# Attention with relative bias and a mixture of adapters: K and V of a head pair in one transfer each, re-aligned by GpSimd casts

## The chip, the cores and the metric

The kernel runs on one core of a Trainium2 chip. The metric is the device time of one execution in microseconds (us); the shown median is over three runs. The engines are TensorE (PE, with its weight loads as PEld), VectorE (DVE), ScalarE (ACT), GpSimd (POOL) and SyncE (SP), which here only issues transfers. The profile is one execution taken by the hardware profiler.

## The reference

Eight batches, eight heads, 576 positions, head dimension 64, all in float32. Each head's scores get a bias that depends on the distance of the two positions; the attention output, laid out as 4608 rows of 512, goes through a mixture of eight rank-16 adapters of which each row uses two.

```python
scores = scale * np.matmul(q, k.transpose(0, 1, 3, 2))
bucket = np.where(is_small, n, large)          # n = |i - j|, 32 buckets
scores = scores + bias_table[bucket].transpose(2, 0, 1)[None]
attn = np.exp(scores - scores.max(-1, keepdims=True))
attn = attn / (attn.sum(-1, keepdims=True) + 1e-09)
x = np.matmul(attn, v)                         # then (4608, 512)
logits = x @ w_gate                            # two best of 8, softmax over the two
out = x + sum(w[:, e] * ((x @ A[e]) @ B[e]) for the two chosen e)
```

## The kernel before, in words

The work goes over 32 head pairs (4 per batch). The 576 positions of a head are 512 in four tiles of 128 (the body) and 64 at the end (the tail). The two heads of a pair stand side by side in 128 columns, so that one transpose serves both; the tails of two heads stand in the two halves of the partitions.

For each pair i: K, Q and V of both heads are loaded as float32 (`kf`, `qf`, `vf`). GpSimd casts them to bfloat16 (`ck_` into `kb`, `cq_` into `qb`, `cv_` into the tiles `vn`, which have a column of ones for the row sums). PE transposes `kb` and `qb` into the PSUM tile `kqps` (`T_pe`), DVE copies it to `kqT` (`T_ev`). PE makes the scores in five parts `qk(i, c)`: four of body keys against body queries, the fifth with the tails of keys and queries, for which the bias (`Hk`, `MT`) is added by matmuls. ACT takes the exponential of each part (`softmax_exp`, 128 x 1024 in, `p` out): 160 such instructions in all. DVE multiplies the exponentials of the bias into a band around the diagonal with two instructions per pair, `p` times `M` (`band`: 128 x 1536 and 128 x 1024, called "bands" below). PE multiplies `p` with `vn` and the tail values `vt` (`pv`), DVE normalizes (`norm1`, `norm2`: `rc` and `x`).

The tails are loaded per batch: `tf` holds those of K and of Q, `vtf` those of V; GpSimd casts them into `tl` (`ct_`) and `vt` (`cvt_`), PE transposes `tl` (`tT_pe`) and makes the scores of tails against tails (`tt_pe`), ACT their exponential (`ptt`). After the fourth pair of a batch the mixture follows: transposes, projection `zf`, the gate chain (`df`, `mk`, `ex`, `sm`, `gate`, of which GpSimd does `df`, `sm`, the product with `ex` and `gate`), `zt` on GpSimd, output `o`. The last batch's mixture is written out separately (`final`), with its gate chain on DVE.

The bias comes from a table: `buckets_of` and `onehot` on DVE, a small matmul `g`, its exponential on ACT and its scaled copy on DVE into `gg`, a store to DRAM (`g_d`), and loads from there that shear it (`Mr`, four of them, and `Hk`), of which DVE makes `M` and `MT`.

Nothing runs in the order in which it is written. Each piece of work is added to a list with an engine, a planned cost in ns, what it depends on, and a due time, to which the table `OFF` adds an offset by key. A planner then lays all of it out engine by engine, earliest due time first among what could start, with planned costs and latencies, and the instructions are emitted in that order; each engine then works strictly in its order. The planner models that a band and a GpSimd instruction exclude each other (`o.sb`, `sb_free`), and it lets each GpSimd instruction wait for one of the two last DVE instructions planned ahead of it (`tie`). Its costs for the GpSimd casts are 560 ns for 512 elements a partition.

Rings of buffers: `kf`, `qf`, `vf` five each, `kb` and `qb` three, `vn` four, `vt` and `tl` two by batch.

Of the kernel before, what the change touches and what calls it, by code (L numbers as in the profile page):

```python
# [10 lines left out]
FP32 = mybir.dt.float32  # L11
# [16 lines left out]
def kernel(  # L28
# [66 lines left out]
    class Op:  # L95
# [5 lines left out]
    WARM2 = 14  # L101
    YIELD = 50
    LATE = 700
# [4 lines left out]
        "lv0": 3.3, "lt0": 28.6, "lvt0": -4.6, "lm0": -27.85, "lm1": -4.85, "lm2": -0.55, "lm3":  # L108
        -2.75, "lh": 1.85, "MT": -1.05, "M0": 4.6, "M1": -8.15, "M2": -2.45, "lw": 2.9, "lwb": -3.8,
        "cv": 11.2, "ct_": -2.35, "cvt0": -5.7, "cvt1": -0.3, "tT0": -2.4, "tT1": -14.4, "tt_":  # L110
        -0.4, "ttx_": -37.4, "qk4_": 0.95, "bd0": -8.7, "bd1": 1.7, "pv00": -6.85, "pv01": -831.15,
        "pv02": -813.15, "pv03": -768.1, "pv04": -778.35, "pv05": -11.85, "na0": -256.25, "nb0":
        -294.1, "pv10": -7.2, "pv11": -712.45, "pv12": -659.3, "pv13": -671.35, "pv14": -747.35,
        "pv15": -8.55, "na1": -52.05, "nb1": -20.35, "lq1": 0.5, "lv1": 1.25, "lt1": -0.5, "lvt1":
        -2.65, "ck": 2.25, "cq": 5.5, "Tk": -9.6, "Tq": -8.8, "Te": -231.7, "qk0": -2.95, "qk1":
        -2.7, "qk2": -7.95, "qk3": -3.95, "lk2": -6.2, "lq2": -15.45, "lv2": 2.2, "qk4": -4.9,
        "lk3": -0.2, "lq3": -1, "lv3": 1, "mx00": -6.7, "mx01": -2.9, "me0": -18, "mx10": -7.25,
        "me1": -29.1, "mt": -3.9, "mte0": -28.55, "mte1": -9.75, "zm0": -5.95, "zm1": -13.05,
        "zem0": -4.4, "zm2": -7.4, "zm3": -6.75, "zem2": -14.75, "gmxm": 37.4, "gdfm": 3.8, "gmkm":
        -9.5, "gexm": -0.4, "gsmm": -11.4, "gmem": 0.75, "grsm": -3.9, "ggtm": 2.6, "gzm0": -5.4,  # L120
        "zTm": -26.15, "zTem": -0.85, "o0": -10.7, "oe0": -23.05, "ost": 6.9, "o2": -3.25, "oe2":
        -0.7, "lq4": -0.5, "lv4": -6.8, "ct0": -2.05, "ct1": 2.35, "tt": -19.35, "ttx": 11.25,
        "lk5": -8.6, "lq5": 6.65, "lv5": 0.65, "lt": 0.15, "lvt": 9.7, "lk": 0.95, "lq": -0.7, "lv":
        0.65, "zt0": -5.25, "zet0": 0.55, "gdft": 0.35, "grst": -7.3, "ggtt": -3.15, "zTt": -13.1,
        "zTet": 1.35, "ot0": -8.95, "ot1": -11.55, "ote": -1.85, "mx00L": -7.55, "mx01L": -4.9,
        "me0L": 3.75, "mx10L": -2.15, "mx11L": -7.65, "me1L": -11, "mtL": -7.95, "mte0L": 4.45,
        "mte1L": -0.45, "zm0L": -15.45, "zm1L": 0.35, "zem0L": 12.15, "zm2L": -9.15, "zm3L": -8.35,
        "zem2L": -1.45, "gmxmL": -6.1, "gdfmL": 3.5, "gmkmL": -14.7, "gexmL": -4.4, "gsmmL": -0.5,
        "gmemL": 5.7, "grsmL": -0.25, "ggtmL": 4.25, "gzm0L": 0.5, "gzm2L": 6.45, "zTmL": -1.8,
        "o0L": 2, "ostL": -6.65, "o2L": 2, "bdL0": -1.9, "bdL1": -0.2, "pvL01": -1.55, "pvL02":  # L130
        -1.7, "pvL03": -0.75, "pvL05": 0.75, "naL0": 3.3, "nbL0": -0.1, "pvL10": -4.7, "pvL11":
        5.65, "pvL12": 1.6, "pvL13": -0.25, "pvL14": -12.7, "pvL15": -0.55, "naL1": -11.25, "nbL2":
        -19.15, "nbL3": -0.7, "fT00": -28.7, "fE00": 15.55, "fEt00": -1.5, "fEt01": -0.5, "fz0":
        0.2, "fw0": -1.45, "fT10": -1.65, "fE10": -13.6, "fEt10": -2.05, "fEt11": 0.45, "fz1": -12,
        "fw1": -4, "fT20": -31.55, "fE20": -2.65, "fEt20": 4.2, "fEt21": -12.8, "fz2": -12, "fT30":
        -39.65, "fE30": 2.65, "fT32": -15.3, "fE32": 0.55, "fEt30": 3.25, "fEt31": 0.25, "fz3": -12,
        "fw3": -4, "gdfL": -5.5, "gmkL": -3.7, "gexL": -3.65, "gsmL": -32.3, "grsL": -3.35, "ggtL":
        -3.1, "fze0": -3.4, "fze2": -0.65, "fze4": -9.95, "fx1": -0.75, "fx3": 0.15, "fx4": 1,
        "fw2": -4,
# [39 lines left out]
    bk = cp.tile([NB, 512], BF16, tag="bk")  # L179
    oneh = cp.tile([NB, 512], FP32, tag="oneh")  # L180
# [29 lines left out]
    def nat_dma(i, h, key, src):  # L210
        b, hp = divmod(i, HP)
        if h == 0:
            stg[(i, key)] = ldp.tile([128, 4, 2, D], FP32, name=key, tag=key)
        SY.dma_start(out=stg[(i, key)][:, :, h, :],
                     in_=src[b, 2 * hp + h, 0:S4, :].rearrange("(g p) d -> p g d", p=128))

    def k0_dma(h):
        if (0, "kf") not in stg:
            stg[(0, "kf")] = ldp.tile([128, 4, 2, D], FP32, name="kf", tag="kf")
        if h is None:  # L220
            AC.dma_start(out=stg[(0, "kf")][:, 0], in_=k[0, 0:2, 0:128, :].rearrange("h p d -> p h d"))
        else:
            SY.dma_start(out=stg[(0, "kf")][:, 1:4, h, :],
                         in_=k[0, h, 128:S4, :].rearrange("(g p) d -> p g d", p=128))
# [7 lines left out]
    def tail_dma(b, w, e, en):  # L232
        if w == 0 and e == 0:
            stg[(b, "tf")] = ldp.tile([128, 2, HP, D], FP32, name="tf", tag="tf", bufs=2)
        EN[en].dma_start(out=stg[(b, "tf")][e * 64:(e + 1) * 64, w],
                     in_=(k, q)[w][b, :, S4:, :].rearrange("(c e) p d -> e p c d", e=2)[e])

    def vtail_dma(b, e):
        if e == 0:
            stg[(b, "vtf")] = ldp.tile([128, HP, D], FP32, name="vtf", tag="vtf", bufs=2)  # L240
        SY.dma_start(out=stg[(b, "vtf")][e * 64:(e + 1) * 64],
                     in_=v[b, :, S4:, :].rearrange("(c e) p d -> e p c d", e=2)[e])

    def load(i):
        t0 = 5.0 * i
        nk = 0.0 if i < 2 else max(4500, 8000 + 980 * (t0 - 17))
        nv = 0.0 if i < 1 else max(8000, 8000 + 980 * (t0 - 12))
        dk = t0 - 14 if i > 5 else -76 + 8 * i if i > 1 else -88
        dv_ = t0 - 8 if i > 4 else -64 + 8 * i if i else -80
        pre = [g_("ck", i - 5), g_("cq", i - 5), g_("cv", i - 5)]  # L250
        ke = str(i) if i < 6 else ""
        if i:
            R["lk", i] = [add("SP", 505, lambda h=h: nat_dma(i, h, "kf", k), pre[:1], dk + .01 * h,
                              nb=nk, dma=600, key="lk" + ke) for h in range(2)]
        else:
            R["lk", 0] = [add("ACT" if h is None else "SP", 450, lambda h=h: k0_dma(h), (),
                              -69 if h is None else -90, dma=300 if h is None else 450)
                          for h in (None, 0, 1)]
        R["lq", i] = [add("SP", 510, lambda: q_dma(i, "SP"), pre[1:2], dk + .02 if i else -95, nb=nk,
                          dma=780, key="lq" + ke if i else None)]  # L260
        R["lv", i] = [add("SP", 505, lambda h=h: nat_dma(i, h, "vf", v), pre[2:], dv_ + .01 * h,
                          nb=nv, dma=600, key="lv" + ke) for h in range(2)]

    def loadt(b, due):
        n = 0.0 if b == 0 else 14000.0 if b == 1 else 8000 + 980 * due
        ke = str(b) if b < 2 else ""
        en = "SP" if b else "ACT"
        for w in range(2):
            for e in range(2):
                R["lt", b, w, e] = add(en, 610, lambda w=w, e=e: tail_dma(b, w, e, en), [g_("ct", b - 2)],  # L270
                                       (due if b > 1 else (-60, -45)[b]) + .01 * e, nb=n, dma=400, key="lt" + ke)
        for e in range(2):
            R["lvt", b, e] = add("SP", 610, lambda e=e: vtail_dma(b, e), [g_("cvt", b - 2)],
                                 (due + 3 if b > 1 else (-58, -34)[b]) + .01 * e,
                                 nb=n + 3000 if b else 9300, dma=400, key="lvt" + ke)

    def ck_(i, e):
        kq[(i, 0)] = ntp.tile([128, 4, 2, D], BF16, name="kb", tag="kb")
        bcopy(EN[e], kq[(i, 0)], stg.pop((i, "kf")))

    def ck0_(w):
        if w == 0:
            kq[(0, 0)] = ntp.tile([128, 4, 2, D], BF16, name="kb", tag="kb")
        s = slice(0, 1) if w == 0 else slice(1, 4)
        PL.tensor_copy(kq[(0, 0)][:, s], stg[(0, "kf")][:, s])

    def T0_pe(w):
# [3 lines left out]
        for j in ((0,), range(4), (1, 2, 3))[w]:  # L291
            PE.transpose(ps[:, w % 2, j * 128:(j + 1) * 128], kq[(0, w % 2)][:, j], ident)
# [15 lines left out]
    def ct_(b, e, h):  # L308
        z = slice(h * 64, (h + 1) * 64)
        bcopy(EN[e], tls[b % 2][z, :, :, z], stg[(b, "tf")][z])  # L310
        if h:
            stg.pop((b, "tf"))
# [935 lines left out]
```

## Time and profile before

| what | value |
|---|---|
| median of 3 runs | 210.38 us (210.02 to 212.13) |
| the profiled execution's own time | 210.69 us |
| its span, first to last instruction | 208.9 us |
| PE, DVE, ACT, POOL busy | 180.3, 171.8, 163.0, 102.9 us |
| granted clock of TensorE, mean | 0.975 |
| POOL instructions | 212 |
| DMA packets, moved | 99649, 39.82 MB |
| of these under 512 B | 87448 |
| K loads on SP | 62 of 128 KB, 4.1 us to landing (median) |
| V loads on SP | 64 of 128 KB, 3.8 us |
| Q loads on SP | 32 of 256 KB, 3.7 us |

How to read the profile: "busy" is the time in which an engine had an instruction in work; issuing transfers and waiting for semaphores are not counted. A line of groups gives source line, engine, operation, output and input tiles with their shapes, the count, the busy time in us, the mean of one in ns, the idle time of the engine just ahead of these instructions, and what ended most of it. All instructions of DVE and POOL carry line L65, that of a recording helper, so they are told apart by their tiles. A line in order of time begins with the start and the length in us; what stands in brackets is the idle time ahead of it and what ended it.

### The profile page before, as it was taken

What the parts mean: (1) busy time and instruction counts of PE and PEld (TensorE: products, weight loads), DVE (VectorE), ACT (ScalarE), POOL (GpSimd) and SP (SyncE); (2) the same over time, 40 slices, a digit from 0 to 9 for tenths busy, and PEclk for the clock granted to TensorE, in tenths of its full rate; (3) what the DMA queues carried; (4) which work ended last, traced back from release to release, by engine and by line L of the source; (5) the groups of instructions that cost most, each with busy time, mean ns of one, the idle gap of its engine ahead of it and who ended that gap; (6) DMA issues with size and microseconds to landing.
All of it is one profiled execution on the core that took longest, in us unless ns stands there. A gap on an engine that the chain in (4) does not pass through costs nothing.

```text
span 208.9 us, 7237 instructions
## 1 busy us (share of the span) xinstructions
PE 180.3 (86%) x2858; PEld 128.3 (61%) x2890; DVE 171.8 (82%) x428; ACT 163.0 (78%) x191; POOL 102.9 (49%) x212
## 2 busy tenths in 40 slices
PE   6838687999999996999998989999999999999660
PEld 3425555777667675666676656667776767669420
DVE  4218578688999979999899989999889999999760
ACT  2348489799999977798889977998989987994350
POOL 7552435646555866729546445654566563001200
PEclk9985999999999999999999999999999999999996
DMA  5949787879787998989768996799789922202057
GB/s 143 258 107 256 160 221 157 178 181 235 167 197 179 272 277 202 237 225 280 184 178 199 264 269 160 184 299 270 174 219 242 287 52 100 104 3 55 0 218 234
DMA packets 99649, 39.82 MB, mean 191 GB/s; under 512 B 87448, under 2 KB 96664, under 8 KB 99616
## 3 DMA queue, kind: packets, MB, share of 16 engines
q1 hardware_dynamic: 96656, 38.17, 71.4%
q10 hardware_dynamic: 2960, 1.20, 2.4%
q8 instruction: 22, 0.36, 0.7%
q14 instruction: 11, 0.09, 0.2%
HBM read 29.90 MB, written 9.45 MB: 188 GB/s over the span
## 4 chain that ended last, share of the span: by engine, by line
PE 40%; DVE 32%; DMA 11%; ACT 6%; issue 3%; POOL 2%; SPq 1%; ACTq 1%; POOLq 0%; DVEq 0%
DVE p L65 12%; PE pv L416 9%; PE sc L362 7%; ACT p L389 5%; PE kqps L349 5%; DVE x L65 4%; DMA kf<-in_k_dram 4%; DVE zf L65 3%; DVE kqT L65 3%; DMA Hk<-g_d 3%; PE pv L425 2%; DMA tf<-in_k_dram 2%; PE sc L567 2%; DVE xT L65 2%; PE sc L367 2%
## 5 line engine op out<-in xcount | busy, mean ns | idle before, releaser
L389 ACT ACTIVATE p<-sc 128x1024 bf16<-128x1024 f32 x160 | 151.2, 1039 | 22.9 <-PE sc L362 9.8
L65 DVE TENSOR_TENSOR p<-p,M 128x1536 bf16<-128x1536 bf16 x64 | 54.6, 853 | 2.7 <-ACT p L389 1.7
L416 PEld LDWEIGHTS <-p 128*128 128x128 bf16 x1024 | 37.8, 98 | 16.1 <-issue 6.7
L362 PE MATMUL sc<-kqT 64*128 64x512 bf16 x256 | 44.5, 396 | 3.7 <-ACT p L389 3.6
L416 PE MATMUL pv<-vn,p 128*128 128x65 bf16 x1024 | 42.6, 195 | 5.4 <-DVE kqT L65 1.6
L65 DVE TENSOR_TENSOR x<-pv,rc 128x320 bf16<-128x320 f32 (+1 forms) x65 | 31.2, 483 | 1.2
L65 POOL CAST kb<-kf 128x512 bf16<-128x512 f32 (+2 forms) x33 | 21.2, 643 | 19.9 <-DMA kf<-in_k_dram 5.1
L65 DVE COPY kqT<-kqps 128x1024 bf16<-128x1024 bf16 (+3 forms) x34 | 22.1, 653 | 7.2 <-PE kqps L349 4.7
L65 POOL CAST qb<-qf 128x512 bf16<-128x512 f32 x31 | 21.8, 702 | 10.4 <-PE sc L362 5.1
L65 POOL CAST vn<-vf 128x512 bf16<-128x512 f32 x32 | 19.7, 616 | 9.1 <-DVE p L65 2.7
L362 PEld LDWEIGHTS <-kqT 64*128 64x128 bf16 x256 | 11.3, 94 | 15.7 <-issue 7.1
L420 PE MATMUL pv<-vn,p 128*128 128x65 bf16 x256 | 18.3, 194 | 0.5 <-ACT p L389 0.5
L425 PE MATMUL pv<-vt,p 128*128 128x65 bf16 x256 | 18.3, 194 | 0.0
L65 DVE RECIPROCAL rc<-pv 128x5 f32<-128x5 f32 x64 | 12.0, 187 | 6.1 <-PE pv L425 5.6
L65 DVE TENSOR_TENSOR o<-sc,x 128x1024 f32<-128x1024 f32 x12 | 14.6, 1215 | 0.2
L349 PE MATMUL kqps<-ident,kb 128*128 128x128 bf16 x124 | 12.1, 220 | 2.7 <-DVE rc L65 1.2
L65 POOL CAST tl<-tf 64x512 bf16<-64x512 f32 x16 | 11.3, 707 | 5.7 <-DVE p L65 2.2
L425 PE MATMUL pv<-vt,ptt 128*128 128x65 bf16 x64 | 12.4, 194 | 1.0 <-ACT ptt L341 1.0
L367 PE MATMUL sc<-tlT,kqT 128*128 128x128 bf16 x128 | 12.7, 222 | 0.5 <-ACT p L389 0.4
L420 PEld LDWEIGHTS <-p 128*128 128x128 bf16 x256 | 12.2, 98 | 0.9 <-ACT p L389 0.9
L349 PEld LDWEIGHTS <-kb 128*128 128x128 bf16 x124 | 7.5, 97 | 8.3 <-DVE x L65 2.9
L425 PEld LDWEIGHTS <-p 128*128 128x128 bf16 x256 | 12.0, 98 | 0.0
(128 smaller groups left out, 268.8 us busy)
## 6 DMA issues: line engine op xcount, KB each, us to landing
qf<-in_q_dram SPq DMA_DIRECT2D x32, 256.0 KB, 3.7
vf<-in_v_dram SPq DMA_DIRECT2D x64, 128.0 KB, 3.8
kf<-in_k_dram SPq DMA_DIRECT2D x62, 128.0 KB, 4.1
out_dram<-o SPq DMA_DIRECT2D x14, 512.0 KB, 4.3
vtf<-in_v_dram SPq DMA_DIRECT2D x16, 64.0 KB, 3.4
tf<-in_k_dram SPq DMA_DIRECT2D x14, 64.0 KB, 3.4
tf<-in_q_dram SPq DMA_DIRECT2D x14, 64.0 KB, 2.9
out_dram<-ot SPq DMA_DIRECT2D x6, 128.0 KB, 2.8
```

The lines of the kernel that those rows point to most:

```text
L65: self.inst = f(*a, **k)
L349: PE.transpose(ps[:, w, j * 128:(j + 1) * 128], t[:, j], ident)
L362: PE.matmul(sc[:, h * 512:(h + 1) * 512], lhsT=t[s, 0, c * 128:(c + 1) * 128], rhs=t[s, 1, :], start=True, stop=True)
L367: PE.matmul(sc[:, g * 128:(g + 1) * 128], lhsT=t[:, 0, g * 128:(g + 1) * 128], rhs=tt[:, 1, hp, :], start=(g == 0), stop=True, skip_group_ ...
L389: AC.activation(probs[(i, c)], st.pop((i, c, "sc")), ACT.Exp, scale=scale)
L416: PE.matmul(acc[:, s, :], lhsT=p[:, o:o + 128], rhs=vn[:, part, h, :], start=(part == 1 and s == 0), stop=False, skip_group_check=True)
L420: PE.matmul(acc[:, 4, :], lhsT=p[:, g * 128:(g + 1) * 128], rhs=vn[:, g, h, :], start=False, stop=False, skip_group_check=True)
L425: PE.matmul(acc[:, s, :], lhsT=l, rhs=vt[:, hp, h * D1:(h + 1) * D1], start=False, stop=True, skip_group_check=True)
L567: PE.matmul(ps[:, k_], lhsT=st[(b, "m", "zT")][:, t + k_, :], rhs=Bb, start=True, stop=not last)
```

## The change

K of a pair (both heads, 1152 rows of 64 numbers that lie one after the other in DRAM) is loaded by one transfer into a tile of 128 partitions and nine slots: row m x 128 + p goes to slot m of partition p. V likewise. The first head's body fills slots 0 to 3; its tail is the lower half of slot 4. The second head starts in the upper half of slot 4, so that each of its tiles lies in the upper half of one slot and the lower half of the next. The casts set this right: `body` has one cast for the first head on 128 partitions and two for the second, each of which writes 64 partitions from the other 64. The V tails come from the same tile with two small casts per pair (`vt_`), so the loads of `vtf` go. K and Q tails have tiles of their own (`tk`, `tf`), each with two loads and two casts per batch; K tails are so read a second time.

The opening's loads follow one list `FIRST` for SP; `Mr` and `Hk` are issued by SP, ACT keeps the bias table, two parts of the first K and the store of `g_d`. The table `g` is made 256 wide and not 512, the rest of `gg` is filled with constants; the second block of warm-up transposes (`warm2`) goes. The first pair transposes Q ahead of K. The exponentials of pairs 0 to 2 are ordered anew. K has six load buffers, and its loads are due 26 ahead of the pair and not 14. The offsets `OFF` are new throughout, with keys of their own for the first eight pairs. Planned costs are 310 for a cast of 256 elements and 130 for one of 64.

```diff
+    FIRST = ("q0 k0 q1 k1 t0 v0 z m0 h q2 k2 m1 v1 q3 k3 m2 v2 q4 k4 v3 m3 k5 "
+             "k6 k7 t1 q5 v4 w q6 v5 k8 q7 v6 k9 v7").split()
+    DUE = {n: -90.0 + .5 * j for j, n in enumerate(FIRST)}
+    KB, VB = 6, 5
...
-    def nat_dma(i, h, key, src):
+    def nat_dma(i, key, src, m0=0, m1=9, e=SY):
         b, hp = divmod(i, HP)
-        if h == 0:
-            stg[(i, key)] = ldp.tile([128, 4, 2, D], FP32, name=key, tag=key)
-        SY.dma_start(out=stg[(i, key)][:, :, h, :],
-                     in_=src[b, 2 * hp + h, 0:S4, :].rearrange("(g p) d -> p g d", p=128))
+        if (i, key) not in stg:
+            stg[(i, key)] = ldp.tile([128, 9, D], FP32, name=key, tag=key, bufs=KB if key == "kf" else VB)
+        e.dma_start(out=stg[(i, key)][:, m0:m1], in_=src[b, 2 * hp:2 * hp + 2].rearrange(
+            "h s d -> (h s) d").rearrange("(m p) d -> p m d", p=128)[:, m0:m1])
...
+    def body(o, f, w, g0=0, g1=4):
+        if w == 0:
+            PL.tensor_copy(o[:, g0:g1, 0, 0:D], f[:, g0:g1])
+        elif w == 1:
+            PL.tensor_copy(o[H0, g0:g1, 1, 0:D], f[H1, 4 + g0:4 + g1])
+        else:
+            PL.tensor_copy(o[H1, g0:g1, 1, 0:D], f[H0, 5 + g0:5 + g1])
...
-    def cv_(i, e):
+    def cv_(i, w):
         vnb[i] = vns[i % 4]
-        bcopy(EN[e], vnb[i][:, :, :, 0:D], stg.pop((i, "vf")))
+        body(vnb[i], stg[(i, "vf")], w)
+
+    def vt_(i, e):
+        b, hp = divmod(i, HP)
+        z = (H0, H1)[e]
+        PL.tensor_copy(vts[b % 2][z, hp, e * D1:e * D1 + D], stg[(i, "vf")][z, 4 + 4 * e])
...
-        x = add("ACT", 620, lambda: AC.activation(gg[:, 0, :], st["g"], ACT.Exp), [g], -97)
-        y = add("DVE", 610, lambda: DVE.tensor_scalar(gg[:, 1, :], st["g"], 1.0 / scale, None, op0=ALU.mult),
-                [g, x], -97)
+        y = add("DVE", 335, lambda: DVE.tensor_scalar(gg[:, 1, ga:gz], st["g"][:, 0:255], 1.0 / scale, None,
+                                                      op0=ALU.mult), [g], -98)
+        x = add("ACT", 400, lambda: AC.activation(gg[:, 0, ga:gz], st["g"][:, 0:255], ACT.Exp), [g, y], -98)
...
-        ms_ = [add("SP" if hp else "ACT", 450, lambda hp=hp: mr(SY if hp else AC, 2 * hp, 2 * hp + 2),
-                   [d], (-98, -57, -49, -41)[hp], dma=1000, key=f"lm{hp}") for hp in range(HP)]
-        R["Hk"] = add("ACT", 600, hk, [d], -97, dma=1600, key="lh")
+        ms_ = [add("SP", 450, lambda hp=hp: mr(SY, 2 * hp, 2 * hp + 2),
+                   [d], DUE[f"m{hp}"], dma=1000) for hp in range(HP)]
+        R["Hk"] = add("SP", 600, hk, [d], DUE["h"], dma=1600)
...
-            R["ck", i] = add(e[0], CC[e[0]], lambda i=i, e=e: ck_(i, e[0]),
-                             R["lk", i] + [g_("Tk", i - 3)], t0 - 10, key="ck")
+            cs = [add("PL", 310, lambda i=i, w=w: ck_(i, w), R["lk", i] + old, d + .01 * w,
+                      key=f"ck{w}" + sx) for w in range(3)]
...
+        cs = [add("PL", 310, lambda i=i, w=w: cv_(i, w), R["lv", i] + [R["vn", i % 4], g_("pv", i - 4, 1)],
+                  t0 - 2 + .01 * w, key=f"cv{w}" + sx) for w in range(3)]
+        vt = [add("PL", 130, lambda i=i, e=e: vt_(i, e), R["lv", i] + [R["vz", b % 2], g_("pv", i - 8, 1)],
+                  t0 - 1 + .01 * e, key=f"vt{e}" + sx) for e in range(2)]
...
+    seq = [(i, c) for i in range(2) for c in range(4)] + [(2, 0), (0, 4), (2, 1), (1, 4), (2, 2), (2, 3), (2, 4)]
+    seq += [(i, c) for i in range(3, NPAIR) for c in range(5)]
```

## The prediction

> **What bounds the kernel now.** I read the page's first two parts, then the windows by stage, then ACT's order of time, then GpSimd's groups by shape.
>
> ```profile
> span 208.9 us, 7237 instructions
> PE 180.3 (86%) x2858; PEld 128.3 (61%) x2890; DVE 171.8 (82%) x428; ACT 163.0 (78%) x191; POOL 102.9 (49%) x212
> ```
>
> ```profile
> 17.46:60.30 42.84, 37.14 (x618) 27.18 (x625) 34.65 (x73) 36.88 (x42) 23.09 (x42) 0.96 0.84 194
> 60.30:109.00 48.70, 45.16 (x740) 32.64 (x749) 44.86 (x100) 41.97 (x49) 29.30 (x54) 1.00 0.89 224
> 109.00:155.00 46.00, 43.23 (x736) 31.40 (x741) 42.82 (x97) 40.45 (x47) 26.42 (x55) 1.00 0.88 228
> ```
>
> Columns of the windows: length, then PE, PEld, DVE, ACT, POOL busy, clock, DMA share, GB/s. In the middle PE and DVE are busy 92 to 94% of the time, ACT 86 to 88%, GpSimd 57 to 60%. No engine is free but GpSimd. ACT in order of time shows the opening and the pace:
>
> ```profile
> 8.76 0.60 ACTq L235 DMA_DIRECT2D tf<-in_q_dram  x1
> 9.41 1.02 ACT L389 ACTIVATE p<-sc 128x1024 bf16<-128x1024 f32 x1 [3.16 <-DMA tf<-in_k_dram]
> 9.50 0.74 ACTq L665 DMA_DIRECT2D g_d<-gg  x1
> 12.47 0.48 ACTq L668 DMA_DIRECT2D Mr<-g_d  x1
> 13.51 6.52 ACT L389 ACTIVATE p<-sc 128x1024 bf16<-128x1024 f32 x7 [3.08 <-issue]
> 26.84 9.27 ACT L389 ACTIVATE p<-sc 128x1024 bf16<-128x1024 f32 x10 [3.14 <-PE sc L362]
> 189.36 1.02 ACT L389 ACTIVATE p<-sc 128x1024 bf16<-128x1024 f32 x1 [0.35 <-PE sc L375]
> ```
>
> ACT's queue stops twice for its own DMA issues (3.16 and 3.08 us), and the bias rows g_d leave only at 9.50. The 11th of 160 exponentials starts at 26.84 and the last ends at 190.38: 150 in 163.5 us, 5.45 us a head pair. The closing is the 18.5 us after that. GpSimd, by shape (busy, mean ns), then one meeting of a cast with DVE's band multiply:
>
> ```profile
> L65 POOL CAST qb<-qf 128x512 bf16<-128x512 f32 x31 | 21.8, 702 | 10.4 <-PE sc L362 5.1 <-PE pv L425 1.8 <-DVE xTt L65 1.1
> L65 POOL CAST vn<-vf 128x512 bf16<-128x512 f32 x32 | 19.7, 616 | 9.1 <-DVE p L65 2.7 <-DMA out_dram<-o 1.8 <-DMA vf<-in_v_dram 1.3
> L65 POOL CAST vt<-vtf 64x256 bf16<-64x256 f32 x16 | 7.9, 497 | 6.2 <-DMA vtf<-in_v_dram 5.0 <-DVE p L65 0.6
> L65 POOL COPY sel<-ident 64x64 bf16<-64x64 bf16 x4 | 1.0, 259 | 0.2
> ```
>
> ```profile
> 31.26 1.09 POOL L65 CAST qb<-qf 128x512 bf16<-128x512 f32 x1 [2.65 <-PE sc L362]
> ```
>
> ```profile
> 31.20 0.68 DVE L65 TENSOR_TENSOR p<-p,M 128x1024 bf16<-128x1024 bf16 x1
> ```
>
> The cast started 0.06 us into the band and took 1.09 us instead of its usual 0.61: it ends 0.47 after the band, so it ran only once the band was over, but for 0.14 us. A cast and a band exclude each other; a meeting gives back about 0.14.
>
> [...] followers start about 0.06 us before the one ahead ends (169.08 against 168.51 + 0.61), those that wait for their predecessor's semaphore about 0.06 after it. [...] the page counts 87448 packets under 512 B now.
>
> **The change part by part.** The sum is made against the profiled execution, 210.69 us (span 208.9, 1.8 around it), 0.3 above the median 210.38.
>
> *Casts on GpSimd (the largest part).* Now a pair has three casts of 128x512, 3 x 0.61 = 1.83. In the new layout rows 64 to 127 of slots 4 to 8 hold the second head shifted by half a tile, so K takes one cast of 128x256 and two of 64x256, V the same and two of 64x64 for its tail. Prices: 64 partitions cost what 128 do (tl 64x512 is 0.61 undisturbed, like kb 128x512), 256 elements 0.40 (the undisturbed vt rows, 0.40 and 0.41), 64 elements 0.24 (the sel copies). A pair: 6 x 0.40 + 0.61 + 2 x 0.24 = 3.49. Per batch, tails 2 x 0.61 + 2 x 0.40 = 2.02 become 4 x 0.40 = 1.60, so 0.51 becomes 0.40 a pair. The gate steps stay at 0.69 a pair (2.18 a batch, 1.21 for each two batches' tails). A pair: 3.03 now, 4.58 then. Over the kernel +1.66 x 32 - 0.42 x 8 = +50 us: GpSimd goes from 103 to about 153 busy, 73% of the span, before any blocking.
>
> A price that the trace doesn't show: a cast from partitions 64-127 to 0-63. Below: 0.40, since the work is the same. Above: 0.80, if it had to move twice. I take 0.40.
>
> [...] To 4.58 come gaps: some 13 instructions a pair, of which a third wait for the predecessor's semaphore (three partial writes of a tile are ordered that way): 13 x (0.35 x 0.06 - 0.65 x 0.06) = -0.23. Then the two bands, 0.96 + 0.68 = 1.64, in which GpSimd stands still, less 0.14 for each meeting, two to four a pair: -0.28 to -0.56. 4.58 - 0.23 + 1.64 - 0.42 = 5.57 us a pair, within 5.43 to 5.71, with GpSimd never waiting for anything else. Now it is 3.03 + 1.64 = 4.7 at most, under the pace of 5.45; then it is just over it. GpSimd becomes the bound. Even the busiest engine now stands 6 to 8% of the middle idle; a late GpSimd finds its waits mostly fulfilled, so I add 4%: 5.57 / 0.96 = 5.80, +0.35 a pair. Its casts are queued in order, so a late K cast holds the transposes on PE (in order too) and everything behind them there, and a late df holds ACT's ex with the exponentials behind it (ACT waited 4.5 us for df already). The first three pairs have casts made in the opening, and the last casts come a pair ahead of their use: 26 pairs x 0.35 = +9.1 us. Bands stretched on DVE are inside this.
>
> *Opening list.* The two 512-wide passes for g (1.04 each) become 256 wide, and the wm block of 14 transposes goes: g is done near 4.8, gg on DVE (half of 0.67) and ACT (about 0.4) near 5.6, and g_d is issued then and not at 9.50: -3.9. Mr and Hk go to SP, whose earlier issues (q0, k0 twice, q1, k1, four tails, v0, q2: eleven of about 0.5) end near 7; it waits there for g_d until about 8.6. Mr lands 4.3 later, M takes 0.55, and the first band starts at 13.6 and not 17.46. Behind the waiting SP stand k2 and later loads, needed by GpSimd at 15: k2 lands near 14.5, just covered. ACT has no tail loads in its queue: from about 8.3 eight exponentials at 0.93 run to 16. GpSimd from 4.99: K0 1.7, q1 0.6, K1 1.2, tails 1.6, three memsets 1.8, V0 1.3, q2 0.6, a V0 piece and K2 1.6, together 10.4 plus small waits, so kqT of pair 2 is there near 18.3 and the 9th exponential at 19, the 11th at 20.9: -5.9. Between the bands' 3.9 and this I take -4.9.
>
> *Transfers.* SP issues 62 + 64 + 16 fewer halves, about 75 of 0.5 us, off the path: nothing. K tails are read twice: 64 rows x 64 heads = 4096 more packets. A packet of q1 takes 71.4% x 16 x 208.9 / 96656 = 24.7 ns on average, so at most 6.3 us on each of 16 engines; the share of 0.89 in the middle becomes 0.92. Hidden behind loads issued up to five pairs ahead; without that cover at most +6. POOL's waits for K loads now (5.1 us) go, but GpSimd is what is late next.
>
> *Closing, other offsets.* The closing's instructions are the same in kind; small swaps of its order cost or bring under 0.5. I take 0.
>
> Sum: 210.7 + 9.1 - 4.9 = 214.9 in a profiled execution, 214.5 as a median.
>
> **Rivals.**
> (a) GpSimd's idle half takes the casts. For it: 49% busy, and K casts are made almost two pairs ahead. Against it: 4.58 + 1.64 = 6.2 before credits. If all four meetings of a pair give back their 0.14 and the 4% doesn't arise, GpSimd needs 5.43 a pair, the pace stays at 5.45, and only the opening shows: 210.4 - 4.9 = 205.5. This is the other side; it decides where GpSimd and bands together stay under 5.45 a pair. Chance 0.24.
> (b) GpSimd follows, but the transfers are late: shares of 0.89 with whole slices at 9, longer transfers that must land complete, V behind K in SP's order. The opening's -4.9 and the +6.3 of the packets: 211.8. Chance 0.10.
> (c) Casts across partitions are dear: 4 a pair x 0.40 more x 26 = +42, about 256. Nothing in the trace shows such a cast. Chance 0.07.
> [...]
>
> **How the numbers follow.** The forecast, 214.5, has 0.59. Its ends: 5.43 without the 4% gives -0.5 - 5.9, about 204; 6.2 / 0.96 in 16 of the 26 pairs gives +16 - 4.9, about 222, and partly dearer shifted casts (0.45) 5 more. I give 205 to 226, which takes in (a) and (b) and leaves (c) out. A measurement of this kernel tells about 1% from no change. Faster by over 1%: (a), 0.24. Within 1%: (b) and a little of the forecast, 0.13. Slower: 0.63.
>
> **What would show it.** Right: GpSimd busy over 150 us, its casts 0.40 and 0.24 when alone; POOL at 80% or more in the middle windows with PE and DVE down to about 88%; PE's transposes waiting for POOL kb and pv for vn; the first band near 13.6, the 11th exponential near 21; 103700 packets. Wrong: POOL under 70% in the middle with PE still over 92% (then (a)), POOL waiting for kf or vf landings (b), shifted casts over 0.5 (c), or an opening that still waits for Mr at 17.

## The result, and the profile after

The changed kernel takes 225.94 us (median of 4 runs, 223.87 to 226.55), the kernel before on the same chip 210.66: ratio 1.070, interval 1.061 to 1.079. Runs that were disturbed are left out of every ratio here, so a ratio need not be the quotient of two medians. The page's head after, to be held against that of before:

```profile
span 224.4 us, 7370 instructions
PE 189.5 (84%) x2876; PEld 131.5 (59%) x2876; DVE 171.7 (77%) x430; ACT 163.6 (73%) x191; POOL 168.8 (75%) x406
```

DVE and ACT have the same work as before. GpSimd went from 102.9 us in 212 instructions to 168.8 in 406. PE is busy 9.2 us longer though it has 14 transposes less; up to 5 us of that can go with its clock, below. The windows by stage (length, then PE, PEld, DVE, ACT, POOL busy, clock, DMA share, GB/s):

```profile
13.50:60.00 46.50, 36.34 (x515) 25.80 (x515) 30.27 (x63) 33.20 (x36) 34.20 (x78) 0.87 0.96 213
60.00:109.00 49.00, 43.07 (x683) 29.95 (x682) 39.62 (x88) 35.98 (x43) 42.06 (x99) 0.95 0.89 212
109.00:155.00 46.00, 42.48 (x705) 30.65 (x706) 40.38 (x90) 38.35 (x44) 38.89 (x92) 1.00 0.85 216
```

In the middle GpSimd is busy 85 to 86% (42.06 of 49.00, 38.89 of 46.00), PE 88 to 92%, DVE 81 to 88%. No engine is full. GpSimd's casts by shape (busy, mean ns, then idle time ahead):

```profile
L65 POOL CAST vn<-vf 64x256 bf16<-64x256 f32 x64 | 30.8, 481 | 4.5 <-DVE p L65 1.7 <-POOL qb L65 0.9 <-DVE rc L65 0.2
L65 POOL CAST kb<-kf 64x256 bf16<-64x256 f32 x62 | 27.5, 443 | 8.2 <-issue 1.7 <-DVE p L65 1.7 <-DVE rc L65 0.7
L65 POOL CAST vt<-vf 64x64 bf16<-64x64 f32 x64 | 25.0, 390 | 2.6 <-POOL qb L65 0.6
L65 POOL CAST kb<-kf 128x256 bf16<-128x256 f32 x31 | 14.4, 464 | 4.1 <-DVE rc L65 2.0 <-DMA kf<-in_k_dram 0.4 <-DVE kqT L65 0.3
```

The shifted 64x256 casts are not dearer than the unshifted 128x256 ones; all the means stand over 0.40 and 0.24, because casts that meet bands take longer (one of 64x256, begun at 14.25, 0.03 us into a band, took 1.20). The idle times in these lines carry almost no DMA: K's transfers are 0.4 us of it.

ACT in order of time gives the opening and the pace:

```profile
6.50 0.54 ACTq L698 DMA_DIRECT2D g_d<-gg  x1
7.25 1.02 ACT L426 ACTIVATE p<-sc 128x1024 bf16<-128x1024 f32 x1 [1.62 <-PE sc L399]
21.31 1.02 ACT L426 ACTIVATE p<-sc 128x1024 bf16<-128x1024 f32 x1 [4.37 <-PE sc L399]
22.49 1.94 ACT L426 ACTIVATE p<-sc 128x1024 bf16<-128x1024 f32 x2 [0.15 <-PE sc L412]
201.83 2.85 ACT L426 ACTIVATE p<-sc 128x1024 bf16<-128x1024 f32 x3 [0.19 <-PE sc L399]
```

The exponential at 21.31 is the 9th of all. The 11th is the second of the two at 22.49 and starts at 23.41 (26.84 before); the last ends at 204.68 (190.38). So the difference of the two profiled executions splits into opening -3.4, middle +17.7 (30 pairs at 6.04 us and not 5.45: 181.3 against 163.5), closing +1.2 (19.7 against 18.5).

One place shows a part of how the middle is lost. ACT, DVE and GpSimd around 80 us:

```profile
84.09 0.24 ACT L539 ACTIVATE ex<-df 128x40 f32<-128x40 f32 x1 [3.94 <-POOL df L65]
```

```profile
78.52 1.75 DVE L65 TENSOR_TENSOR p<-p,M 128x1536 bf16<-128x1536 bf16 x2
81.92 0.16 DVE L65 MAX8 zf<-zf 128x8 f32<-128x8 f32 x1
```

```profile
82.52 0.40 POOL L65 CAST vn<-vf 64x256 bf16<-64x256 f32 x1
82.99 0.40 POOL L65 CAST tl<-tk 64x256 bf16<-64x256 f32 x1
83.45 0.40 POOL L65 CAST vn<-vf 128x256 bf16<-128x256 f32 x1
83.81 0.25 POOL L65 TENSOR_TENSOR df<-zf 128x40 f32<-128x40 f32 x1
```

The maxima that `df` needs end at 82.1. GpSimd has casts ahead of `df` in its order and reaches it at 83.81; ACT, in order, holds its exponentials behind `ex` for 3.94 us. GpSimd's casts account for the 1.7 us from 82.1 to 83.81; the rest passed before the maxima were there. From the first exponential of that pair to the first of the next it is 10.6 us.

### The profile page after: what moved, and what is told of

Read it like the earlier page. It is cut to its first block, busy times and chain, and to the rows that moved or that the text cites. A ratio compares the mean times of both kernels' runs of the same rounds, so it can differ in the third digit from the quotient of the medians.

```text
span 224.4 us, 7370 instructions
## 1 busy us (share of the span) xinstructions
PE 189.5 (84%) x2876; PEld 131.5 (59%) x2876; DVE 171.7 (77%) x430; ACT 163.6 (73%) x191; POOL 168.8 (75%) x406
## 2 busy tenths in 40 slices
DMA packets 102498, 40.87 MB, mean 182 GB/s; under 512 B 90296, under 2 KB 99512, under 8 KB 102464
## 4 chain that ended last, share of the span: by engine, by line
PE 32%; DVE 32%; POOL 12%; DMA 9%; issue 6%; ACT 4%; SPq 1%; DVEq 0%; POOLq 0%; ACTq 0%
DVE p L65 12%; PE pv L453 8%; PE sc L399 6%; DVE x L65 4%; PE kqps L386 4%; ACT p L426 4%; DVE o L65 4%; DVE kqT L65 4%; POOL vn L65 4%; POOL kb L65 3%; DMA kf<-in_k_dram 3%; DMA out_dram<-o 3%; DMA qf<-in_q_dram 2%; PE pv L462 2%; DVE rc L65 2%
## 5 line engine op out<-in xcount | busy, mean ns | idle before, releaser
L65 DVE TENSOR_TENSOR p<-p,M 128x1536 bf16<-128x1536 bf16 x64 | 55.6, 869 | 2.3 <-ACT p L426 0.5
L65 POOL CAST kb<-kf 64x256 bf16<-64x256 f32 (+4 forms) x99 | 43.6, 440 | 12.9 <-DVE rc L65 2.7
L65 POOL CAST vn<-vf 64x256 bf16<-64x256 f32 (+1 forms) x96 | 44.9, 468 | 7.2 <-DVE p L65 3.2
L453 PE MATMUL pv<-vn,p 128*128 128x65 bf16 x1024 | 44.5, 196 | 6.0 <-DVE kqT L65 3.7
L399 PE MATMUL sc<-kqT 64*128 64x512 bf16 x256 | 47.3, 407 | 2.4 <-ACT p L426 1.4
L453 PEld LDWEIGHTS <-p 128*128 128x128 bf16 x1024 | 38.9, 99 | 16.1 <-issue 9.9
L65 POOL CAST vt<-vf 64x64 bf16<-64x64 f32 x64 | 25.0, 390 | 2.6 <-POOL qb L65 0.6
L65 POOL CAST qb<-qf 128x512 bf16<-128x512 f32 x31 | 20.5, 662 | 3.0 <-DVE p L65 1.7
L457 PE MATMUL pv<-vn,p 128*128 128x65 bf16 x256 | 18.3, 194 | 0.0
L386 PE MATMUL kqps<-ident,qb 128*128 128x128 bf16 x124 | 12.9, 231 | 1.8 <-POOL qb L65 1.8
L404 PE MATMUL sc<-tlT,kqT 128*128 128x128 bf16 x128 | 13.6, 233 | 0.0
L410 PE MATMUL sc<-kqT,tlT 128*128 128x512 bf16 x32 | 13.4, 418 | 0.0
L457 PEld LDWEIGHTS <-p 128*128 128x128 bf16 x256 | 12.3, 98 | 1.1 <-issue 0.9
```

Source lines behind the costliest of these rows:

```text
L65: self.inst = f(*a, **k)
L386: PE.transpose(ps[:, w, j * 128:(j + 1) * 128], t[:, j], ident)
L399: PE.matmul(sc[:, h * 512:(h + 1) * 512], lhsT=t[s, 0, c * 128:(c + 1) * 128], rhs=t[s, 1, :], start=True, stop=True)
L404: PE.matmul(sc[:, g * 128:(g + 1) * 128], lhsT=t[:, 0, g * 128:(g + 1) * 128], rhs=tt[:, 1, hp, :], start=(g == 0), stop=True, skip_group_ ...
L410: PE.matmul(sc[:, 512:1024], lhsT=tt[:, 0, hp, :], rhs=t[:, 1, :], start=True, stop=False, skip_group_check=True)
L453: PE.matmul(acc[:, s, :], lhsT=p[:, o:o + 128], rhs=vn[:, part, h, :], start=(part == 1 and s == 0), stop=False, skip_group_check=True)
```

## The experiments

Three theories stood at the start. G: GpSimd's amount of work, with the bands that shut it out, sets the pace. O: the written order and the waits between engines do. T: the longer transfers do. Later came P: the plan's prices for the small casts are too short, so that its order is late at run time. Ratios are to the kernel before on the same chip, with 95% intervals; the changed kernel's is 1.070 [1.061, 1.079].

**1. Work out of the changed kernel.**

```diff
     def body(o, f, w, g0=0, g1=4):
         if w == 0:
-            PL.tensor_copy(o[:, g0:g1, 0, 0:D], f[:, g0:g1])
-        elif w == 1:
...
+            PL.tensor_copy(o[:, g0:g1, :, 0:D], f[:, 2 * g0:2 * g1].rearrange("p (g h) d -> p g h d", h=2))
```

> Changed kernel with its loads, opening and order kept, but the 128x512 of K and of V each cast by one unshifted instruction of 0.61 us on GpSimd instead of three of 0.40 (the second head's rows are then not aligned: that part of the computation is left out). GpSimd's busy time falls by about 55 us. Theory G (GpSimd's own work, with the bands that shut it out, sets the pace): the pace comes back to 5.5 us a pair and only the opening's gain is left, 206 to 210 us. Theory O (the written order and the waits between engines, not GpSimd's amount of work): 218 us or more. Theory T (the longer contiguous transfers come too late): 220 us or more.

Measured: 214.7 us, 1.014 [1.009, 1.018]. GpSimd fell from 168.8 to 117.2 us busy. Four fifths of the loss is gone, and T can hold for no more than the rest, since the transfers are the changed ones. The added waits of the casts that fall away fall away with them, so this run alone doesn't part the work from the waits (experiments 4 to 7 do). And 214.7 is neither G's 206 to 210 nor O's 218: the pace from the 11th to the last exponential is 5.71 us a pair, not the 5.45 of before, so something of the changed order stays.

**2. The same work put into the kernel before.**

```diff
-        bcopy(EN[e], kq[(i, 0)], stg.pop((i, "kf")))
+        PL.tensor_copy(o[:, :, 0, 0:D], f[:, :, 0, :])
+        for z in (slice(0, 64), slice(64, 128)):
+            PL.tensor_copy(o[z, :, 1, 0:D], f[z, :, 1, :])
...
```

> Kernel before, its loads, opening and order kept, but each cast of K and V on GpSimd is cut in three (128x256 and twice 64x256), the V tails and the K and Q tails in smaller pieces: the mix of GpSimd's instructions is that of the changed kernel, all aligned, result unchanged. Theory G: the pace goes from 5.45 to about 6.0 us a pair without any gain in the opening, 222 to 230 us. Theory O or T: 211 to 214 us, since the order and the transfers are those of before.

Measured: 228.1 us, 1.075 [1.069, 1.080], with the loads, the opening and the order of before and no shift between partitions. The page's line:

```profile
PE 190.7 (84%) x2890; PEld 132.1 (58%) x2890; DVE 173.7 (77%) x428; ACT 163.7 (72%) x191; POOL 159.5 (70%) x402
```

The cut into small casts alone gives a loss as large as the whole, with the number of added waits of before. Its pace from the 11th to the last exponential (27.35 to 207.80) is 6.02 us a pair, that of the changed kernel 6.04.

**3. Aligned loads in the changed kernel.** K and V by one transfer a head, V tails by batch, one cast of 128x512 each.

```diff
...
+            for h in range(2):
+                if g == 0 or h == (m0 == 6):
+                    e.dma_start(out=t[:, g:4, h, :],
+                                in_=src[b, 2 * hp + h, g * 128:S4, :].rearrange("(g p) d -> p g d", p=128))
...
```

> Changed kernel with the opening and order kept, but K and V loaded aligned, one transfer for each head (and V tails per batch), and one cast of 0.61 us for each of K and V; result unchanged. Theory G: 205 to 209 us, faster than before by the opening's gain, if the order after it, made for other cast times, fits. Theory O: 218 us or more. Theory T: as G, but the experiment with one unshifted cast stays slow.

Measured: 215.7 us, 1.017 [1.012, 1.022]. The interval overlaps that of experiment 1, where K and V came contiguous: one transfer for a pair neither costs nor brings anything that shows. G's 205 to 209 was missed again, by 7 us or more. The stretch from the 11th to the last exponential, of the kernel before and of this one:

```profile
26.84:190.38 163.54, 151.95 (x2542) 110.33 (x2569) 149.46 (x331) 146.31 (x166) 86.79 (x168) 1.00 0.78 198
22.95:194.89 171.94, 157.97 (x2582) 112.38 (x2580) 146.84 (x331) 146.12 (x167) 86.81 (x182) 0.99 0.76 190
```

GpSimd is as busy as before (86.81 against 86.79 us), and yet the pace is 5.73 us a pair and not 5.45. The new order, which was planned for the small casts, costs some 8 us in the middle even where GpSimd has no more to do than before; in this execution the sooner opening gives back 3.9 us of them.

**4. The planner's added waits.** Each GpSimd instruction waits for one of the two DVE instructions planned last ahead of it. Here they are left out.

```diff
-        if o.after is not None:
+        if False:
             tc.add_manual_dep(PL.inst.ins, o.after.inst.ins.name, mybir.DependencyInfo(
```

> Changed kernel without the planner's added waits of GpSimd's casts on VectorE's instructions (the written order on each engine is kept). Theory G: 223 to 229 us, since GpSimd has the same work and the same bands shut it out. Theory O, in the form that the added waits hold GpSimd up: 212 to 219 us, and GpSimd's share in the middle rises from 85% to over 90%.

Measured: 218.8 us, 1.033 [1.027, 1.038]. So 3.7 points of the 7.0 go with the waits; G's 223 to 229 was missed, and the time is O's in the form that the added waits hold GpSimd up. Windows of this kernel:

```profile
60.00:109.00 49.00, 42.98 (x706) 30.49 (x707) 41.25 (x94) 36.24 (x44) 45.34 (x104) 1.00 1.01 244
109.00:155.00 46.00, 42.69 (x707) 30.39 (x704) 40.89 (x91) 39.93 (x46) 39.82 (x93) 1.00 0.86 215
```

GpSimd is busy 93% in the first (86% with the waits), 87% in the second (85%). The pace is 5.81 us a pair (11th exponential at 23.20, last end at 197.50).

**5 to 7. The same waits left out elsewhere:** of the kernel before, of experiment 2, of experiment 3. The edit is that of experiment 4.

> Kernel before without the planner's added waits of GpSimd on VectorE, order kept. A control for the 7 us that the changed kernel gained without them. If the added waits cost whatever the load: 207 us or less. If they cost only where GpSimd has little slack (theory G with waits): 209 to 212 us, no difference from before.

Measured: 212.4 us, 1.009 [1.006, 1.011]: without them the kernel before is a little slower, and not faster.

> Kernel before with the changed kernel's mix of small casts (228.1 us with the added waits) and without the added waits. Theory G with waits (the larger part is the wait on VectorE, which a late GpSimd pays in full, and lateness breeds lateness): 217 to 221 us, some 8 us less. Work alone: 226 to 229 us.

Measured: 224.4 us, 1.052 [1.039, 1.065], against 1.075 with them; the time lies between the two expectations. The ratio rests on two runs, 221.1 and 223.8 us. The gain is less than the changed kernel's, in direction the same.

> Changed kernel's opening and order with aligned loads and one cast of 128x512 for each of K and V (215.7 us with the added waits), now without the added waits. If the remaining 5 us over before are the added waits: 209 to 211 us. If they are the written order itself (stalls near 37 and 75 us in which ACT and PE wait for VectorE, with GpSimd half idle): 214 to 216 us.

Measured: 216.7 us, 1.026 [1.018, 1.034], against 1.017 with them. The waits help slightly or do nothing where GpSimd has slack (5, 7) and cost where it has little (4, and with a wide interval 6). They are not what keeps the light version of the changed kernel above before. Put together ("light": one cast of 128x512 for each of K and V):

| order, casts | with the waits | without |
|---|---|---|
| before, light | 1 | 1.009 |
| before, all in pieces | 1.075 | 1.052 |
| changed, light | 1.017 | 1.026 |
| changed, all in pieces | 1.070 | 1.033 |

So the pieces cost 7.5 points in the order of before and 5.3 in the changed one. Without the waits they cost 4.3 points in the order of before, and in the changed one 0.7, where the intervals overlap. The same stretch as above, of experiment 7 and of experiment 4:

```profile
23.46:195.52 172.06, 157.93 (x2582) 112.06 (x2580) 148.87 (x330) 146.14 (x167) 97.53 (x182) 0.99 0.75 189
23.20:197.50 174.30, 156.66 (x2574) 111.17 (x2573) 147.79 (x330) 146.03 (x167) 153.33 (x344) 1.00 0.79 191
```

56 us more of GpSimd's busy time, being shut out included, lengthen it by 2.2 us only. In the changed order it is thus the pieces together with the waits that cost; that GpSimd's work alone costs there is not shown.

**8. The opening alone**, put into the kernel before with its planned order kept:

```diff
-        st["g"] = msp.tile([H, 512], FP32, name="g", tag="ms")
+        st["g"] = msp.tile([H, 256], FP32, name="g", tag="ms")
...
-            for _ in range(WARM2):
-                PE.transpose(t, ident, ident)
...
-        EN[en].dma_start(out=stg[(b, "tf")][e * 64:(e + 1) * 64, w],
+        SY.dma_start(out=stg[(b, "tf")][e * 64:(e + 1) * 64, w],
```

> Kernel before, with its own loads, casts and order from the third pair on, and only the changed kernel's opening: the passes for g 256 wide, no second block of 14 transposes, g_d issued right after gg, tails and the first Mr and Hk on SP's queue. If the opening's gain is real and kept: the 11th exponential starts near 23 and not 26.8, and the time is 206 to 208 us. If it is given back in the next pairs, as in the run with aligned loads (where pairs 2 to 5 took 25.8 us for 20.5): 209 to 212 us.

Measured: 0.9915 [0.987, 0.996], which with the 210.4 us of before would be about 208.6, between the two expectations. But this ratio rests on 7 of the 20 runs; the median of all 20 is 211.1 us, that of all 39 runs of the kernel before beside them 210.95. A gain in time is not shown. ACT in order of time:

```profile
24.15 6.52 ACT L389 ACTIVATE p<-sc 128x1024 bf16<-128x1024 f32 x7 [4.10 <-PE sc L362]
188.79 1.02 ACT L389 ACTIVATE p<-sc 128x1024 bf16<-128x1024 f32 x1 [0.35 <-PE sc L375]
```

The 11th exponential starts 2.7 us sooner than before, the last ends at 189.81 and only 0.6 sooner in this execution: most of the gain is given back along the way.

**9 to 11. Other prices in the plan.**

```diff
-            cs = [add("PL", 310, lambda i=i, w=w: ck_(i, w), R["lk", i] + old, d + .01 * w,
+            cs = [add("PL", 400, lambda i=i, w=w: ck_(i, w), R["lk", i] + old, d + .01 * w,
...
-        vt = [add("PL", 130, lambda i=i, e=e: vt_(i, e), R["lv", i] + [R["vz", b % 2], g_("pv", i - 8, 1)],
+        vt = [add("PL", 236, lambda i=i, e=e: vt_(i, e), R["lv", i] + [R["vz", b % 2], g_("pv", i - 8, 1)],
```

> Changed kernel, its planner given the durations that the trace shows for GpSimd's casts (0.40 for 0.31 and 0.33, 0.236 for 0.13, 0.612 for 0.56), so that order and added waits are made for them; due times and offsets kept, though they were made for the old prices. Theory P (the plan counts a pair's casts as 2.7 us where they take 3.5, so its order and its waits on VectorE are late at run time): 216 to 221 us with the waits in. Theory G (amount of work): 223 to 229 us whatever the plan.

> The same new plan without the added waits. Theory P: within 2 us of the run with them, since waits planned for the right durations come true. If the waits cost by themselves wherever GpSimd is busy: 5 us or more less than with them.

> Kernel before with the small casts (228.1 us), its planner given their durations (1.20 for the three of K and of V, 0.80 and 0.94 for the tails' pieces), added waits kept. Theory P: 217 to 222 us. Theory G: 225 to 230 us.

Measured: 243.5 us (1.155 [1.148, 1.162]), 246.9 (1.167 [1.158, 1.176]) and 247.2 (1.168 [1.159, 1.177]). All expectations were missed. With the measured prices under offsets made for others, each kernel is worse by 18 to 28 us than the same work in its own order (225.9, 218.8, 228.1). A changed price moves the whole order, so these three say nothing yet on P; they say what a misfitting order costs.

**12 and 13. Is there a threshold?** In the kernel before, K's cast alone cut in three; then V's cast and the V tails.

> Kernel before with K's cast alone cut in three (0.59 us more a pair, a third of the whole set's 1.66), V and tails as before. If there is a threshold (GpSimd with the bands stays under the pace of 5.45 us a pair: 3.03 + 0.59 + 1.64 = 5.26): 211 to 213 us. If every added microsecond lengthens the chain (K's casts stand before PE's transposes): a third of 16 us or more, 216 to 219 us.

Measured: 213.1 us, 1.0075 [1.005, 1.010].

> Kernel before with V's cast cut in three and the V tails in 64x64 pieces (some 1.1 us more a pair), K and the K and Q tails as before; K alone (0.59 us more) cost 1.6 us, all of it (1.66) 16 us. Threshold (GpSimd with the bands passes the pace of 5.45 us a pair only near the end of that scale: 3.03 + 1.1 + 1.64 = 5.8): 216 to 220 us, far more than twice K's. Proportional to the added work, as K alone gave it: 214 to 215.5 us. Then what K and V do together (the rest of the 16) is an interaction.

Measured: 214.6 us, 1.012 [1.005, 1.020]. That is the value of a proportional loss. But the parts add to 2.0%, and all together cost 7.5%: the loss grows faster than the work. Experiment 2 also cut the K and Q tails (0.10 us more a pair by the prices); that was not tried alone, but the same pieces stand in experiment 1, at 1.014. (The added work was stated as 1.1 us a pair; from the prices it is 0.59 for the body and 0.28 for the tails, 0.87.)

**14 and 15. Offsets fitted to the measured prices**, by a search in the planner's model; the second without the added waits.

> Changed kernel, the planner given GpSimd's measured durations, and its offsets fitted anew to them by a search in the planner's own model (planned length 223.7 against 229.8 with the old offsets; the changed kernel plans 203.7 for itself with the too short prices). If the loss was the too short prices and the unfitted order: 210 to 217 us. If GpSimd's work with the bands is what the plan can't hide at the right prices, as its planned length says: 223 us or more.

> The same without the added waits. If they cost because the plan's prices were too short: within 2 us of the run with them. If they cost wherever GpSimd has no slack: 4 to 8 us less, as between the changed kernel with and without them (225.9 and 218.8).

Measured: 236.0 us (1.114 [1.104, 1.125]) and 238.9 (1.128 [1.119, 1.136]). Better than with unfitted offsets, still 10 us above the changed kernel. P gets no support: this order, planned at the right prices, was not better than the one planned at too short ones. It isn't refuted either, since experiment 16 finds the orders of this search slower than its model says even with light casts. The waits cost nothing in this order. The model forbids GpSimd any part of a band, and at true prices spreads the work out; that this is why is not shown.

**16. The opening with a refitted order.** `OFF` is fitted anew in the kernel of experiment 8.

> Kernel before with the changed kernel's opening (0.9915 of before) and its offsets fitted anew by the same search, to GpSimd's measured durations (planned length 198.0, the kernel before plans 195.9 for itself at slightly shorter prices). If a refitted order keeps what the opening brings: 205 to 208 us. If the model's order is no better than the one that came with before: 209 to 215 us.

Measured: 218.0 us, 1.029 [1.023, 1.035], above both expectations. An order that the model puts 1% behind that of before (198.0 against 195.9) is 3% behind on the chip.

**17 and 18. The threshold in the changed order.** Only K, then only V, by one cast (the edit of experiment 1 in `ck_` or in `cv_`).

> Changed kernel with only K cast by one unshifted instruction of 0.61 us (its second head's rows then not aligned, that part of the computation left out), V and the tails as changed: 0.59 us a pair less for GpSimd. With both by one the changed kernel came from 225.9 (1.070) to 214.7 (1.014). Threshold in the changed order too: most of it back, 1.015 to 1.030, 215 to 218 us. Proportional: half of it, 1.040 to 1.048, 220 to 222 us.

> Changed kernel with only V cast by one unshifted instruction (that part of the computation left out), K and the tails as changed. The same amount less as for K alone. Threshold: 1.015 to 1.030. If K's place decides (its casts stand before PE's transposes, V's only before the last products of the pair): V alone brings little, 1.05 or more.

Measured: 216.6 us (1.027 [1.016, 1.037]) and 219.0 (1.036 [1.024, 1.049]). Either half of the added casts taken away brings back more than half of the loss that both account for: 4.3 and 3.4 points of 5.6. A proportional loss would have left 1.042 in both. K's interval excludes that, V's includes it, and V's 1.036 lies above the 1.015 to 1.030 that a threshold was to give: in this order the threshold is supported, not settled.

Against the prediction's own sum for a pair (casts and gate steps plus the bands' 1.64, without credits) the eight kernels, all with the added waits, line up within each order:

| order | us a pair, summed | ratio |
|---|---|---|
| before | 4.67 | 1 |
| before, K in three | 5.26 | 1.0075 |
| before, V and V tails in pieces | 5.54 | 1.012 |
| before, all in pieces | 6.22 | 1.075 |
| changed, K and V by one cast | 5.04 | 1.014 |
| changed, K by one | 5.63 | 1.027 |
| changed, V by one | 5.63 | 1.036 |
| changed | 6.22 | 1.070 |

In the order of before little is lost up to about 5.5, its own pace, and 6% from there to 6.22. In the changed order 1 to 2% are lost from 5.04 to 5.63, and 3 to 4% from there. The sum is a scale and no bound: at 6.22 the changed kernel without the waits ran at 5.81 us a pair. Experiment 1 and the two here have fewer waits along with fewer casts, so in this order it is a threshold of casts and waits together.

## Why the prediction was right in direction and too small

The step that failed is the sum for the middle: +0.35 us a pair, 26 times, from a surcharge of 4% on GpSimd's own time and from new offsets put at nothing. Measured are +0.59 us a pair, 30 times, 17.7 us and not 9.1. Part by part:

- *Casts.* Right. 0.40 and 0.24 when alone, shifted or not; experiment 2 has no shift and the same loss. Rival (c) is out.
- *GpSimd becomes the bound, with a threshold near the pace.* Right in part. The small casts alone give the loss (experiment 2), and it grows faster than the work (2, 12 and 13; 17 in favour, 18 open). But GpSimd did not become full: it is idle 14 to 15% of the two middle windows. In the changed order most of what the pieces cost needs the added waits as well (experiments 3, 4 and 7). Rival (a), that GpSimd's idle half takes it, nearly holds in the order of before for up to about half of the added work (12 and 13: 0.8 and 1.2% lost), not for all of it.
- *"So I add 4%".* Here the sum failed first. GpSimd is busy 80.95 of the 95.00 us of the two middle windows, being shut out included, and idle 15%; without the added waits it is busy 85.16 and idle 10%. At paces of 6.04 and 5.81 its own time is then some 5.2 us a pair (an estimate, share times pace) and not 5.57. The prediction treated a late GpSimd as finding "its waits mostly fulfilled"; it did not count the planner's waits on DVE, which a late DVE makes it pay: between 60 and 155 us its longer waits for DVE are 7.7 us, and 2.5 where the added waits are left out. The added waits cost 0.23 us a pair, 7 us in all (experiment 4). That the pace without them, 5.81, is the 5.80 of the forecast is luck: GpSimd's own time was put too high, its idle time too low, and the same order runs at 5.74 without the waits when the casts are light.
- *Other offsets, "I take 0".* This was said of the closing, and for the middle the new offsets have no term at all. With light casts the changed order runs at 5.71 to 5.74 us a pair (experiments 1, 3 and 7) where that of before ran at 5.45: some 8 us. From profile to profile the 17.7 us come in as 8.5 with the order (before to experiment 7), 2.2 with the pieces (to experiment 4) and 7.0 with the waits (to the changed kernel); 2.2 is within what executions of one kernel differ by. The shares belong to this sequence: in the order of before the pieces alone bring 16.9 (experiment 2), so order, casts and waits don't simply add.
- *PE's clock.* Part of the 7 us can run through it: three stretches after the opening ran at half clock (0.50 to 0.51 granted). Ahead of them PE waited for GpSimd's `tl` (1.4 us), for its `qb` (1.8), and for DVE's `kqT` (2.1), with DVE held for GpSimd's `sm` (2.4). Two of them, in pairs of windows:

```profile
37.90:41.30 3.40, 1.23 (x16) 0.79 (x14) 2.18 (x5) 0.55 (x1) 2.60 (x6) 1.00 0.89 218
41.40:44.80 3.40, 3.40 (x31) 3.12 (x30) 1.61 (x3) 1.62 (x2) 3.08 (x7) 0.50 1.07 245
85.80:89.20 3.40, 1.53 (x35) 1.29 (x34) 2.02 (x6) 1.27 (x2) 3.07 (x10) 0.99 0.73 163
89.20:92.60 3.40, 3.40 (x25) 2.08 (x25) 2.69 (x5) 2.90 (x3) 3.01 (x6) 0.50 1.11 244
```

  PE is busy 1.2 to 1.6 of 3.4 us, then 3.4 us at clock 0.50; the third stretch, from 58.4, is like them (1.59 us busy ahead of it, 3.11 in it). Four transposes take 0.61 to 0.63 us in these stretches (at 58.69 and 43.65) and 0.39 to 0.40 at full clock (88.66 and 83.89), less than twice as long. So at most half of the 9.9 us in which PE is busy in the three is the clock's, 5 us in all (an estimate from these times). What the clock goes by is not shown. A low share of work just ahead was not enough in the kernel of experiment 4:

```profile
51.80:55.20 3.40, 1.17 (x14) 0.72 (x12) 0.79 (x2) 2.26 (x4) 2.96 (x8) 1.00 0.98 229
55.20:58.60 3.40, 3.24 (x62) 2.21 (x62) 2.71 (x6) 3.12 (x4) 3.23 (x6) 1.00 1.10 248
```

  The runs bound the clock's part. The four of the changed kernel had mean clocks of 0.957, 0.957, 0.967 and 0.982 and took 226.2, 226.6, 225.7 and 223.9 us. The four without the added waits had 0.970 to 0.978 and took 218.5 to 219.1, on a chip on which the kernel before was no faster. So the changed kernel at its best clock is still 4.7 us above any of them, and most of what the waits cost isn't the clock.
- *"26 pairs".* Too few: the measured loss is spread over 30. With 0.35 a pair that is 1.4 us; the further 0.24 a pair (6.04 and not 5.80) is 7.2.
- *Opening, -4.9.* Measured -3.4. g_d was issued at 6.50 (5.6 forecast), the first band began at 14.22 (13.6), so the bands gained 3.2. The 9th exponential came at 21.31 and not 19. Part of what held it:

```profile
14.25 1.20 POOL L65 CAST vn<-vf 64x256 bf16<-64x256 f32 x1
15.51 0.95 POOL L65 CAST qb<-qf 128x512 bf16<-128x512 f32 x1
16.52 0.40 POOL L65 CAST vn<-vf 64x256 bf16<-64x256 f32 x1
17.25 1.51 POOL L65 CAST kb<-kf 64x256 bf16<-64x256 f32 x3 [0.33 <-DMA kf<-in_k_dram]
```

```profile
18.82 0.61 PE L386 MATMUL kqps<-ident,kb 128*128 128x128 bf16 x4 [2.50 <-POOL kb L65]
```

  The sooner bands meet casts that stand ahead of the third pair's `kb` and Q's own cast: 1.20 for 0.40, 0.95 for 0.61. PE then waits 2.50 us for `kb`. The prediction summed these casts at their lone prices.
- *Transfers, 0.* Right: 102498 packets (103700 forecast), 90296 of them under 512 B (87448 of 99649 before), so one transfer for a pair didn't make them large; GpSimd's waits for K loads down to about 1 us, experiments 1 and 3 alike. Rival (b) is out.
- *Closing, 0.* Measured +1.2. It was not tried apart.

Against the forecast's terms, 9.1 + 1.4 + 7.2 = 17.7 for the middle, -3.4 for the opening and +1.2 for the closing make the 15.5 us between the two profiled executions. The 7.2 is what was left over, so this sum closes by itself and explains nothing.

What stays open: with light casts the changed order is 1.4 to 1.7% slower than before, though its first band and its 11th exponential come sooner. Stalls like that at 80 us remain in it with GpSimd half idle (in experiment 3 ACT waits 2.5 us for `df` at the same place). Which part of the order costs was not settled, nor why the pieces cost so much less in it without the waits than in the order of before.

## What to carry to other kernels

An engine at half load took added work for little here only until its own time, plus the time in which another engine shut it out, came near the pace (in the order of before, with a pace of 5.45 us a pair, 1.2% were lost at a sum of 5.54 and 7.5% at 6.22): make that sum for the stage in question. Past it, count every wait that was put into the order while there was slack: waits that help slightly at half load cost half of the loss here. Price the new order by itself, with the old work in it: here it cost about as much as the waits, and the forecast had no term for it. An order with fitted offsets belongs to its prices; refitting it in a model that misjudges such orders by some 2% was no repair here.

## What was not expected of the hardware

- The casts' times went by elements a partition and not by partitions: alone, 128x512 and 64x512 took 0.61 us, 128x256 and 64x256 0.40, 128x64 and 64x64 0.23 to 0.24. One 128x512 cut in three so took 3 x 0.40 = 1.20, and a shift by 64 partitions cost nothing (0.40 with it and without).
- TensorE's granted clock fell to 0.50 to 0.51 in three stretches of the changed kernel's middle, each time after 3.4 us in which PE had been busy for 1.2 to 1.6. In the kernel of experiment 4, 1.17 us busy in 3.4 was followed by full clock (1.00), so the busy share just ahead doesn't decide it.
